# Attention and two MLPs on one core: the first MLP's first tile takes ten steps of d_ff before tile two, not six

## The chip, the cores and the metric

One NeuronCore of a Trainium2 chip runs the whole program in one launch. The metric is device microseconds of that core, from launch to end. A profile is one execution with the hardware profiler on.

## What is computed

For 4 batches and 8 heads of 768 positions and 64 dimensions, each chunk of 32 queries attends to 16 positions to its left, its own 32, 8 to its right, and 8 memory positions. The result, as 3072 tokens of 512 values, goes through two MLPs with d_ff = 2048:

```python
scores = scale * np.matmul(q_c, k_full.transpose(0, 1, 3, 2))
a = softmax(scores); out[:, :, c_start:c_end] = np.matmul(a, v_full)
...
h = x @ w_in                                    # first MLP
g = np.where(h > 0.0, h, alpha * (np.exp(np.minimum(h, 0.0)) - 1.0))
x = g @ w_out
...
r = np.maximum(x @ w_in2, 0.0)                  # second MLP
out = (s * (r * r) + b) @ w_out2
```

## The kernel before, in words

**Attention** is cut into 24 units of 128 queries (all heads at once), numbered here from 0 as in the code; the fifth to the eighth are units 4 to 7. For a unit u < 8, step S multiplies q and k (tile psS, L239) and runs the softmax on VectorE and ScalarE (L258 to L266), step P turns the probabilities round on TensorE (psP, L281) into the one tile pt, and step V multiplies them by v (psV, L313) and splits the result into a high and a low part of the first MLP's input: xh (ScalarE, L204) and xl (VectorE, L208). From unit 8 on P is a series of transposes on VectorE (L289), and V of one unit and S of the next share one PSUM tile (psVS). Once the first MLP has begun, psS, psV and psVS come from one and the same PSUM slot (`ps_a`, one buffer): S of unit u+2 cannot start before xl of unit u has been read out of psV.

**The first MLP** works on 6 tiles of 512 tokens (4 units each). All products are three matmuls of rounded parts (L361, L362, L363: high by high, high by low, low by high). A step (t, c) of tile t takes the c-th of 16 blocks of 128 of d_ff: 12 matmuls into psH (first layer, `h1`), then ELU (L392, L393 on ScalarE, L394 on VectorE), the split into gh (L204) and gl (L208), and two steps later 12 matmuls into the four accumulators acc (`out1`). Tile 0 is taken in two pieces: its first `HF` steps come as soon as units 0 to 3 are done, then all 16 steps of tile 1, then the rest of tile 0. Between the pieces the four accumulators of tile 0 are copied out, stored to a scratch tensor (`part_dram`, L427), and later loaded (L413) and added to (L419).

**Weights** come as float64. Each of the 32 loads (raw, L149, 512 KB) is turned into high and low parts by four operations, two on ScalarE (top L158, w L172) and two on VectorE (t L161, w L208). `weights_to` doles these out as micro-steps between the parts of a step.

**Order.** The first steps, up to V of unit 3, stand in a table written by hand (EARLY) and are held in that order. After it, `mlp1_step` writes a step of the MLP and, with `beside`, the next few attention steps and weight micro-steps; the framework then schedules each engine's instructions by its own cost model, and each engine runs its list in order. The list `steps` has 73 attention steps: S0, then S, P, V of each unit to 7 (three per unit), then three per unit. `ready[0]` is 14 and `ready[1]` is 26, so 13 attention steps, from S of unit 5 to P of unit 8, are spread over the first piece of tile 0. The 47 that are left are spread from step (1, `ATT_FROM`) to (3, 8). All loads and stores go through one queue, SP's, in order; a load that waits for its buffer holds up those behind it.

Of the kernel before, what the change touches and what calls it, by code (L numbers as in the profile page):

```python
# [28 lines left out]
NU = B * UPB  # L29
NP = H // 2  # L30
NU0 = 8
HF = 6
ATT_FROM, ATT_END = 10, (3, 8)
MICRO = 8
HN, NT2 = 512, 3
NBLOCK = 10
# [25 lines left out]
def tile_attention_then_two_mlps(ctx, tc, q_in, k_in, v_in, w1, w2, s_in, b_in, out):  # L62
# [270 lines left out]
    def load_x(t):  # L333

        X[t] = xh, xl = x_tiles((t + 1) % 2)
        nc.sync.dma_start(out=f(xl), in_=x_dram[:, :, starts[t] * U:(starts[t] + sizes[t]) * U])
        nc.scalar.activation(out=xh, in_=f(xl), func=AF.Copy)
        sub(xl, f(xl), xh)
# [47 lines left out]
    def h1(t, c):  # L386
        n = sizes[t] * U
        n0 = 2 * U if t == 0 and c in HALF else 0
        ps = HALF.pop(c) if n0 else ps_h.tile([P, 512], F32, tag="h", name="psH")
        h_mm(c, ps, X[t], n0, n)  # L390
        g = one.tile([P, MAXN], F32, tag="g", name="g")
        nc.scalar.activation(out=g[:, :n], in_=ps[:, :n], func=AF.Relu, scale=-1.0)  # L392
        nc.scalar.activation(out=g[:, :n], in_=g[:, :n], func=AF.Exp, scale=-1.0)  # L393
        nc.vector.scalar_tensor_tensor(out=g[:, :n], in0=g[:, :n], scalar=-1.0, in1=ps[:, :n],  # L394
                                       op0=ALU.add, op1=ALU.max)
        G[1, t, c] = split_g(g, n)
# [10 lines left out]
    def put_out(t, c, n):  # L407

        split, t0 = t == 0, starts[t] * U
        if c == HF and split:  # L410
            for m in range(KT):
                PART[m] = big_tile(n, m == 3)
                nc.sync.dma_start(out=PART[m], in_=part_dram[:, m, :n])  # L413
        if c == NF - 1 or c == HF - 1 and split:
            for m, acc in enumerate(ACC[t]):
# [13 lines left out]
    def out1(t, c):  # L429
        n = sizes[t] * U  # L430
        first, last = (c in (0, HF), c in (HF - 1, NF - 1)) if t == 0 else (c == 0, c == NF - 1)
        if first:
# [41 lines left out]
    def prepare_all():  # L474
        for layer in range(2):
            for i in range(NF // 2):
                yield from prepare(layer, i)
# [17 lines left out]
    ready = [min(next(k for k, g in enumerate(steps) if g and g[0] in ((step_V, u), (step_VS, u))) + 2, len(steps)) for u in last_v]  # L495
# [21 lines left out]
    def run_step(group):  # L517
        for st, u in group:
            s = u + (st is step_VS)
            while st in (step_S, step_VS) and nload[0] <= min(s + 1, NU - 1):  # L520
                load_qk(nload[0])
                nload[0] += 1
            while st in (step_S, step_VS) and nload[1] <= s:
                load_v(nload[1])
                nload[1] += 1
            st(u)
# [10 lines left out]
    def weights_to(w, n, ahead):  # L537

        while wnext[0] < min(n, MICRO * NF):
            k, m = divmod(wnext[0], MICRO // 2)  # L540
            load_ws(w, k + 1 + ahead)
            if m == 0:
                wsteps[:] = [split_w(*SLOTS[k], wraw[k])]
            next(wsteps[0])
            wnext[0] += 1
# [40 lines left out]
    def beside(want, weights):  # L586

        w, n, ahead = weights
        n0, d0 = wnext[0], done[0]
        while done[0] < want:  # L590
            run_step(steps[done[0]])
            done[0] += 1
            weights_to(w, n0 + (n - n0) * (done[0] - d0) // (want - d0), ahead)
        weights_to(w, n, ahead)
# [48 lines left out]
    def open_second():  # L643

        z = (NTILE1 + 1) % 2
        halves = iter(range(10))
        for j in (1, 2, 3, 6, 5, 7, 4):
            if j in (6, 5):
                xc = xp.tile([P, 2, 2, HN], F32R, tag=f"{'xh' if j == 6 else 'xl'}{z}", name=f"xc{j}")
                XC[j] = xc[:, 0], xc[:, 1]  # L650
            else:
                XC[j] = high(next(halves)), high(next(halves))
        p2["yr"] = [wps[1].tile([P, 2, HN], F32, tag=f"w1_{c}", name=f"yr{c}") for c in range(4)]
        p2["blocks"] = load_blocks(0)

    def mlp1_step(n_):

        t, c = seq[n_]
        phase[0] = (1 if c < HF else 3) if t == 0 else 2 if t == 1 else 4

        a0, total, k, ks = done[0], 0, 0, 1
        if t == 0 and c < HF:
            a0, total, k, ks = ready[0] - 1, ready[1] - ready[0] + 1, c, HF
        elif spread[0] <= n_ < spread[1]:
            a0, total, k, ks = ready[1], len(steps) - ready[1], n_ - spread[0], spread[1] - spread[0]

        wt = [(w1, 0, 4)] * 2
        if t == 0 and c < HF:
            n0, n1 = 12, 8 * HF + 12
            wt = [(w1, max(n0 + (n1 - n0) * (2 * c + z) // (2 * HF), MICRO * (c + z) - 4), 4) for z in (1, 2)]  # L670
        elif t == 1:
            n0 = 8 * HF + 12
            wt = [(w1, max(n0 + (MICRO * NF - n0) * (2 * c + z) // 28, MICRO * (c + z) - 4), 4) for z in (1, 2)]
        if (t, c) == ATT_END:
            actx.close()
            op.append(mctx.enter_context(tc.tile_pool(name="op2", bufs=2)))
            p2["prep"] = mctx.enter_context(tc.tile_pool(name="prep", bufs=2, reuse_waits="tile"))
            p2["steps"] = prepare_all()
            nc.sync.dma_start(out=s_sb, in_=s_in.to_broadcast([P, 1]))
            nc.sync.dma_start(out=b_sb, in_=b_in.to_broadcast([P, 1]))  # L680
        if t < 2:
            weights_to(w1, MICRO * c + 4, 4)
        if t == NTILE1 - 1 and c == NBLOCK:
            open_second()
        h1(t, c)
        yield
        beside(a0 + total * (2 * k + 1) // (2 * ks), wt[0])
        prepared(t, 2 * c + 1)
        yield
        beside(a0 + total * (2 * k + 2) // (2 * ks), wt[1])  # L690
        prepared(t, 2 * c + 2)
        if t == NTILE1 - 1 and c >= NBLOCK:
            for _ in range(3):
                next(p2["blocks"], None)
        if c == NF - 4 and 1 <= (t or 1) < NTILE1 - 1 and t != 1:
            assert done[0] >= ready[max(t, 1) + 1]
            load_x(max(t, 1) + 1)
        yield

    def prepared(t, n):  # L700

        begin = 2 * (NF * ATT_END[0] + ATT_END[1])
        want = min(NPREP * (2 * NF * t + n - begin) // (2 * NF * (NTILE1 - 1) + 2 * NBLOCK - 2 - begin), NPREP)
        while (t, n) > (ATT_END[0], 2 * ATT_END[1]) and p2["n"] < want:
            next(p2["steps"])
            p2["n"] += 1
# [7 lines left out]
    def single(n_):  # L714
        step = mlp1_step(n_)
        next(step)
        next(step)
        if n_ >= 2:
            out1(*seq[n_ - 2])
        next(step)  # L720

    def pair(n_):
        steps2 = [mlp1_step(n_), mlp1_step(n_ + 1)]
        for k in (0, 0, 1, 0):
            next(steps2[k])
        for k in range(2):
            out1(*seq[n_ - 2 + k])
            next(steps2[1])
# [185 lines left out]
```

## Time and profile before

| | us |
|---|---|
| median of 3 runs | 1088.03 |
| the runs | 1088.59, 1088.03, 1078.59 |
| the profiled execution | 1087.85 |
| its span, first to last instruction | 1086.1 |
| TensorE busy in the span | 1062.0 |

In a row of the trace the times are microseconds from the start of the span. A group gives the start, the time to the end of its last instruction, the engine, the line, the operation, and how many there are; a bracket gives the time for which the engine had stood idle, and what ended it. Matmul durations overlap: the work of a run of matmuls is read from start to start. PEclk is the granted clock of TensorE, 1.00 for 2.4 GHz and 0.50 for 1.2 GHz.

### The profile page before, as it was taken

To read this page: it belongs to the slowest core of one execution; us is meant where nothing else is said; L and a number is where in the kernel's file an instruction comes from. 1 tells how busy PE (TensorE), PEld (TensorE's weight loads), DVE (VectorE), ACT (ScalarE), POOL (GpSimd) and SP (SyncE) were. 2 spreads that over 40 slices of the span, in tenths; PEclk is the share of its full clock that TensorE was granted. 3 is DMA by queue.
4 is the path that set the end of the run, shared out by engine and by line. 5 is a ranking of instruction groups with operands and counts; after the bars stand their busy time and mean duration, and the time that the engine had idled before them with its cause. 6 is when DMAs were issued, how large, how long until landed. Compare 5 with 4: busy or idle time off the path is not lost.

```text
span 1086.1 us, 18733 instructions
## 1 busy us (share of the span) xinstructions
PE 1062.0 (98%) x7466; PEld 865.4 (80%) x7466; DVE 731.9 (67%) x1133; ACT 548.2 (50%) x773; POOL 1.2 (0%) x7
## 2 busy tenths in 40 slices
PE   6899999999999999999999899999999999999998
PEld 5778888878888888888878787788888788888887
DVE  6788558777778777787773155697356696365854
ACT  3677533443434356676763255654355654355542
POOL 0000000000000000000000000000000000000000
PEclk7799999999999999999999999999999999999999
DMA  8886025516325158988932366767766777666673
GB/s 314 333 309 219 11 63 161 177 59 191 109 79 178 50 170 309 334 318 314 332 131 78 126 193 188 245 201 232 231 192 186 243 214 228 208 195 193 201 206 126
DMA packets 94838, 213.02 MB, mean 196 GB/s; under 512 B 9760, under 2 KB 17952, under 8 KB 92704
## 3 DMA queue, kind: packets, MB, share of 16 engines
q1 hardware_dynamic: 94176, 210.79, 60.3%
q8 instruction: 59, 0.97, 0.4%
q10 hardware_dynamic: 576, 1.05, 0.3%
q14 instruction: 27, 0.22, 0.1%
HBM read 164.61 MB, written 47.19 MB: 195 GB/s over the span
## 4 chain that ended last, share of the span: by engine, by line
PE 80%; DVE 9%; DMA 5%; ACT 3%; issue 2%; SPq 0%; ACTq 0%; DVEq 0%
PE psH L361 13%; PE psH L363 12%; PE psH L362 12%; PE psL L362 7%; PE psL L363 7%; PE psL L361 7%; PE acc L361 6%; PE acc L362 6%; PE acc L363 6%; DVE pt L289 2%; DMA hi<-y_dram 2%; DMA raw<-w 1%; DVE g L394 1%; DVE gl L208 1%; PE psVS L313 1%
## 5 line engine op out<-in xcount | busy, mean ns | idle before, releaser
L361 PE MATMUL psH<-xh,w 128*128 128x512 f32 (+1 forms) x392 | 154.8, 395 | 2.3 <-ACT xh L204 1.2
L363 PE MATMUL psH<-xh,w 128*128 128x512 f32 (+1 forms) x392 | 152.4, 389 | 0.0
L362 PE MATMUL psH<-xl,w 128*128 128x512 f32 (+1 forms) x392 | 152.0, 388 | 0.2 <-DVE xl L208 0.2
L361 PE MATMUL acc<-gh,w 128*128 128x512 f32 x384 | 152.0, 396 | 0.0
L362 PE MATMUL acc<-gl,w 128*128 128x512 f32 x384 | 150.7, 392 | 0.0
L363 PE MATMUL acc<-gh,w 128*128 128x512 f32 x384 | 150.5, 392 | 0.0
L394 DVE SCALAR_TENSOR_TENSOR g<-g,psH 128x512 f32<-128x512 f32 x96 | 65.7, 684 | 62.4 <-ACT g L393 61.5
L392 ACT ACTIVATE g<-psH 128x512 f32<-128x512 f32 x96 | 56.7, 591 | 94.0 <-PE psH L363 51.4
L204 ACT ACTIVATE gh<-g 128x512 fp32r<-128x512 f32 x96 | 60.3, 628 | 84.6 <-DVE g L394 84.3
L361 PE MATMUL psH<-hi,hi 128*128 128x512 f32 x240 | 94.0, 398 | 1.3 <-ACT p L765 1.3
L362 PE MATMUL psH<-hi,hi 128*128 128x512 f32 x240 | 93.8, 391 | 0.0
L363 PE MATMUL psH<-hi,hi 128*128 128x512 f32 x240 | 93.7, 390 | 0.0
L815 ACT ACTIVATE g2xl<-g 128x1024 fp32r<-128x1024 f32 x56 | 59.5, 1063 | 60.1 <-PE psL L363 59.9
L361 PEld LDWEIGHTS psH<-xh,w 128*128 128x128 f32 x392 | 74.4, 190 | 18.8 <-ACT xh L204 1.6
L362 PE MATMUL psL<-g2l,hi 128*128 128x512 f32 x224 | 87.4, 390 | 1.2 <-DVE g2l L208 1.2
L208 DVE TENSOR_TENSOR gl<-g,gh 128x512 fp32r<-128x512 f32 x96 | 66.2, 690 | 32.1 <-ACT gh L204 30.5
L363 PE MATMUL psL<-g2xl,hi 128*128 128x512 f32 x224 | 87.1, 389 | 0.0
L362 PEld LDWEIGHTS psH<-xl,w 128*128 128x128 f32 x392 | 74.6, 190 | 15.6 <-DVE xl L208 0.6
L361 PE MATMUL psL<-g2xl,hi 128*128 128x512 f32 x224 | 86.8, 389 | 0.0
L363 PEld LDWEIGHTS psH<-xh,w 128*128 128x128 f32 x392 | 74.3, 190 | 15.5
L361 PEld LDWEIGHTS acc<-gh,w 128*128 128x128 f32 x384 | 72.6, 189 | 16.7 <-ACT pt L204 0.6
L363 PEld LDWEIGHTS acc<-gh,w 128*128 128x128 f32 x384 | 72.5, 189 | 15.7
(108 smaller groups left out, 1847.3 us busy)
## 6 DMA issues: line engine op xcount, KB each, us to landing
hi<-s_dram SPq DMA_DIRECT2D x336, 256.0 KB, 3.0
raw<-w SPq DMA_DIRECT2D x64, 511.8 KB, 6.3
s_dram<-right SPq DMA_DIRECT2D x16, 1024.0 KB, 5.2
kb<-k SPq DMA_DIRECT2D x24, 512.0 KB, 5.7
v<-v SPq DMA_DIRECT2D x24, 512.0 KB, 3.8
s_dram<-left SPq DMA_DIRECT2D x16, 768.0 KB, 4.1
q<-q SPq DMA_DIRECT2D x24, 256.0 KB, 5.3
out<-r SPq DMA_DIRECT2D x24, 256.0 KB, 3.7
```

What stands on the lines that cost most here:

```text
L204: return nc.scalar.activation(out=hi, in_=src, func=AF.Copy)
L208: return nc.vector.tensor_tensor(out=lo, in0=src, in1=f(hi), op=ALU.subtract)
L289: nc.vector.transpose(out=pt[k * CH:(k + 1) * CH, :, rows], in_=sm[rows, :, z, n0:n0 + CH])
L313: keep(nc.tensor.matmul(ps[r % 2 * D:(r % 2 + 1) * D, z, o:o + CH], v[rows, (r * NC + c) * D:(r * NC + c + 1) * D], pt[rows, r, cs], start ...
L361: keep(nc.tensor.matmul(o, sa(a[0]), sb(b[0]), start=first, stop=False, skip_group_check=again))
L362: keep(nc.tensor.matmul(o, sa(a[0]), sb(b[1]), start=False, stop=False, skip_group_check=again))
L363: return keep(nc.tensor.matmul(o, sa(a[1]), sb(b[0]), start=False, stop=last, skip_group_check=again))
L392: nc.scalar.activation(out=g[:, :n], in_=ps[:, :n], func=AF.Relu, scale=-1.0)
L394: nc.vector.scalar_tensor_tensor(out=g[:, :n], in0=g[:, :n], scalar=-1.0, in1=ps[:, :n], op0=ALU.add, op1=ALU.max)
L815: nc.scalar.activation(out=gh, in_=g[:, block], func=AF.Copy)
```

## The change

Tile 0's first piece has ten steps, not six (`HF` is also the number at which its accumulators are put out and begun again), and its second piece six, not ten. The 13 attention steps beside the first piece are spread over nine of its steps (`ks` is `HF - 1`; `min` keeps the tenth from asking for more). The 47 others begin at step 4 of tile 1, not at step 10; that is 42 MLP steps to spread over in place of 40. The weight micro-steps per MLP step are the same (8), and the target of the first piece rises from 60 to 92 of the 128.

```diff
-HF = 6
-ATT_FROM, ATT_END = 10, (3, 8)
+HF = 10
+ATT_FROM, ATT_END = 4, (3, 8)
...
         if t == 0 and c < HF:
-            a0, total, k, ks = ready[0] - 1, ready[1] - ready[0] + 1, c, HF
+            a0, total, k, ks = ready[0] - 1, ready[1] - ready[0] + 1, c, HF - 1
...
-        beside(a0 + total * (2 * k + 1) // (2 * ks), wt[0])
+        beside(a0 + min(total * (2 * k + 1) // (2 * ks), total), wt[0])
         prepared(t, 2 * c + 1)
         yield
-        beside(a0 + total * (2 * k + 2) // (2 * ks), wt[1])
+        beside(a0 + min(total * (2 * k + 2) // (2 * ks), total), wt[1])
```

What stands where now is seen from the scheduled lists. On TensorE, between V of unit 4 (psV) and V of unit 5, there stood before (psH of w_3 is tile 0's step 3, acc of w_0 its step 0; a run of 12 matmuls is cut to its ends):

```order
L363 MATMUL psH<-xh,w_2_686 128x512
L313 MATMUL psV<-pt,v 64x32 x32
L361 MATMUL psH<-xh,w_2_686 128x512
L362 MATMUL psH<-xl,w_2_686 128x512
L363 MATMUL psH<-xh,w_2_686 128x512
L239 MATMUL psS<-kb,q 32x64 x32
L281 MATMUL psP<-ident,sm_106 128x128 x4
L361 MATMUL psH<-xh,w_3_765 128x512
L362 MATMUL psH<-xl,w_3_765 128x512
L361 MATMUL acc_866<-gh,w_0_602 128x512
...
L363 MATMUL acc_869<-gh,w_0_602 128x512
L313 MATMUL psV<-pt,v 64x32 x32
```

and now:

```order
L313 MATMUL psV<-pt,v 64x32 x32
L361 MATMUL acc_810<-gh,w_0_602 128x512
...
L363 MATMUL acc_813<-gh,w_0_602 128x512
L361 MATMUL psH<-xh,w_3_728 128x512
...
L363 MATMUL psH<-xh,w_3_728 128x512
L239 MATMUL psS<-kb,q 32x64 x32
L361 MATMUL psH<-xh,w_3_728 128x512
L362 MATMUL psH<-xl,w_3_728 128x512
L363 MATMUL psH<-xh,w_3_728 128x512
L281 MATMUL psP<-ident,sm_106 128x128 x4
L361 MATMUL acc_810<-gh,w_1_694 128x512
```

Before, three large matmuls stood between V of unit 4 and S of unit 6; now 21 do (12 of acc, 9 of psH). Further on, 12 stand between V of unit 5 and S of unit 7, 11 between V of unit 6 and S of unit 8, and 35 between V of unit 7 and the first matmul of tile 1, where before two of that tile's matmuls came after five.

On SP's queue, from the load of unit 4's v on, before:

```order
L199 DMA v<-v 128x1024
L192 DMA kb<-k 128x1024
L194 DMA q<-q 128x512
L199 DMA v<-v 128x1024
L149 DMA raw_1_675<-w 128x2047
L149 DMA raw_3_677<-w 128x2047
L149 DMA raw_2_679<-w 128x2047
L149 DMA raw_4_681<-w 128x2047
L149 DMA raw_3_695<-w 128x2047
```

and now:

```order
L199 DMA v<-v 128x1024
L149 DMA raw_1_625<-w 128x2047
L149 DMA raw_3_627<-w 128x2047
L149 DMA raw_2_629<-w 128x2047
L149 DMA raw_4_631<-w 128x2047
L192 DMA kb<-k 128x1024
L194 DMA q<-q 128x512
L199 DMA v<-v 128x1024
L149 DMA raw_3_689<-w 128x2047
```

Four weight loads have moved ahead of k and q of unit 6 and v of unit 5.

## Rows read from the trace of the kernel before

**Rows 1.** Page, part 1: busy time, share of the span, instructions.
```profile
PE 1062.0 (98%) x7466; PEld 865.4 (80%) x7466; DVE 731.9 (67%) x1133; ACT 548.2 (50%) x773; POOL 1.2 (0%) x7
```

**Rows 2.** Busy time by stretch: stretch, length, each engine, granted clock, DMA share, GB/s.
```profile
0.00:39.15 39.15, 30.86 (x726) 25.87 (x727) 24.26 (x47) 15.97 (x26) 1.16 (x7) 0.78 0.85 296
39.15:55.16 16.01, 13.05 (x222) 9.69 (x222) 13.91 (x27) 10.99 (x19) 0.00 (x0) 0.79 0.96 381
55.16:81.12 25.96, 24.66 (x352) 19.07 (x346) 22.34 (x42) 19.19 (x33) 0.00 (x0) 1.00 0.84 315
81.12:560.00 478.88, 477.46 (x3933) 391.70 (x3932) 352.30 (x708) 250.51 (x401) 0.00 (x0) 1.00 0.53 182
560.00:645.00 85.00, 81.17 (x347) 65.62 (x346) 34.83 (x42) 33.11 (x49) 0.00 (x0) 0.98 0.37 112
645.00:1086.00 441.00, 434.82 (x1897) 353.47 (x1896) 284.27 (x271) 218.43 (x247) 0.00 (x0) 1.00 0.70 205
```

**Rows 3.** Timeline of TensorE, 41 to 62 us.
```profile
41.39 1.14 PE L313 MATMUL psV<-pt,v 64*64 64x32 f32 x64
...
45.07 0.76 PE L239 MATMUL psS<-kb,q 64*32 64x64 f32 x52 [1.65 <-DVE xl L208]
47.13 0.46 PE L239 MATMUL psS<-kb,q 64*32 64x64 f32 x12 [1.30 <-issue]
47.52 1.11 PE L281 MATMUL psP<-ident,sm 128*128 128x128 f32 x4
48.28 0.78 PE L361 MATMUL psH<-xh,w 128*128 128x512 f32 x1
...
53.33 0.39 PE L361 MATMUL acc<-gh,w 128*128 128x512 f32 x1
...
54.10 1.14 PE L313 MATMUL psV<-pt,v 64*64 64x32 f32 x64
55.16 0.50 PE L363 MATMUL psH<-xh,w 128*128 128x512 f32 x1
...
57.65 0.86 PE L239 MATMUL psS<-kb,q 64*32 64x64 f32 x64
58.44 0.50 PE L361 MATMUL acc<-gh,w 128*128 128x512 f32 x1
...
61.30 0.60 PE L281 MATMUL psP<-ident,sm 128*128 128x128 f32 x4
61.65 0.48 PE L361 MATMUL psH<-xh,w 128*128 128x512 f32 x1
```

**Rows 4.** Busy time by stretch, columns as in rows 2.
```profile
44.00:46.00 2.00, 0.76 (x52) 0.60 (x52) 2.00 (x5) 0.89 (x2) 0.00 (x0) 1.00 1.04 411
46.00:48.00 2.00, 0.87 (x15) 0.70 (x15) 1.06 (x4) 1.66 (x4) 0.00 (x0) 0.62 1.02 391
48.00:50.00 2.00, 2.00 (x7) 1.35 (x7) 2.00 (x4) 1.87 (x4) 0.00 (x0) 0.50 1.04 417
```

**Rows 5.** Timeline of TensorE, around the first matmuls of tile 1, and later.
```profile
79.21 0.73 PE L361 MATMUL psH<-xh,w 128*128 128x512 f32 x2 [1.15 <-ACT xh L204]
...
80.55 0.50 PE L362 MATMUL psH<-xl,w 128*128 128x512 f32 x1 [0.15 <-DVE xl L208]
...
95.04 0.39 PE L361 MATMUL acc<-gh,w 128*128 128x512 f32 x1
...
100.51 0.39 PE L361 MATMUL psH<-xh,w 128*128 128x512 f32 x1
```

**Rows 6.** Timeline of VectorE: xl of units 4 to 7.
```profile
44.37 0.64 DVE L208 TENSOR_TENSOR xl<-psV,xh 128x512 fp32r<-128x512 f32 x1
...
55.93 0.69 DVE L208 TENSOR_TENSOR xl<-psV,xh 128x512 fp32r<-128x512 f32 x1 [1.01 <-ACT xh L204]
...
67.61 0.68 DVE L208 TENSOR_TENSOR xl<-psV,xh 128x512 fp32r<-128x512 f32 x1
...
79.80 0.69 DVE L208 TENSOR_TENSOR xl<-psV,xh 128x512 fp32r<-128x512 f32 x1
```

**Rows 7.** Timeline of TensorE: V of units 6 and 7, and unit 13's.
```profile
64.58 1.14 PE L313 MATMUL psV<-pt,v 64*64 64x32 f32 x64
...
75.57 1.13 PE L313 MATMUL psV<-pt,v 64*64 64x32 f32 x64
...
225.13 0.78 PE L313 MATMUL psVS<-pt,v 64*64 64x32 f32 x38 [1.10 <-DVE pt L289]
```

**Rows 8.** Timeline of SP's queue: k and q of unit 6, v of unit 5.
```profile
30.33 0.33 SPq L192 DMA_DIRECT2D kb<-k  x1
30.71 0.42 SPq L194 DMA_DIRECT2D q<-q  x1
33.46 0.33 SPq L199 DMA_DIRECT2D v<-v  x1
33.84 3.54 SPq L149 DMA_DIRECT2D raw<-w  x6
```

**Rows 9.** DMA queue 8 between 44 and 45 us: packets, MB, share of 16 engines.
```profile
q8 instruction: 1, 0.02, 6.7%
```

**Rows 10.** DMA issues: tile, queue, count, KB each, median us to landing.
```profile
big<-part SPq DMA_DIRECT2D x4, 256.0 KB, 3.6
```

**Rows 11.** Timeline of VectorE: two instructions back to back, a transpose group.
```profile
49.13 0.68 DVE L208 TENSOR_TENSOR w<-t,w 128x512 fp32r<-128x512 f32 x1
49.73 0.68 DVE L259 TENSOR_TENSOR sm<-psS,nmx 128x512 f32<-128x512 f32 x1
...
80.53 3.79 DVE L289 STREAM_TRANSPOSE pt<-sm 32x128 f32<-32x128 f32 x12
```

## The prediction

> **What bounds the kernel now.** I read first the busy times: TensorE works 1062.0 us of 1086.1 us [rows 1], so a change that only moves work can give back at most 24.1 us of idle time, and what lies in half-clock stretches. Then the same by stretch, to see where those lie [rows 2]. Of the idle time 39.15 - 30.86 = 8.3 us comes before the first full 512-column matmul, 3.0 us from there to V of unit 4 being followed by V of unit 5 (39.15 to 55.16), 1.3 us to the first step of tile 1, 1.4 us in the long middle, and 10.0 us after 560 us, where the second MLP is being opened and run. The change touches the second and third stretch and the order in the fourth. The lists of the engines are the same before V of unit 4 but for details, and the same again from tile 2 on, so the first stretch and the last two should stand. Two things make up the second stretch: idle time and clock. Its granted clock is 0.79, while the next is at 1.00 [rows 2].
>
> The timeline of TensorE shows the chain there [rows 3]. S of unit 6 waits 1.65 us for xl of unit 4, because only three large matmuls lie between V of unit 4 and it, and VectorE gets to xl at 44.37 us, 1.84 us after V's end at 42.53 [rows 3, 6]. In the middle of S comes another pause, 1.30 us, put down to issue. Behind the two the granted clock falls from 1.00 to 0.50, by way of 0.62 [rows 4], and stays there until 53.33 us.
>
> **What the change takes away, step by step.**
>
> The wait for xl of unit 4: xl ends at 45.01 us, 2.5 us after V. Now 21 large matmuls stand between V and S. One takes 0.228 us at full clock: from 95.04 to 100.51 us lie 24 of them [rows 5], 5.47 / 24. So 21 are 4.8 us, against 2.5 us: **1.65 us** gone.
>
> The half clock: from 48.28 to 53.33 us eleven matmuls take 5.05 us; at 0.228 they take 2.51 us, so 2.5 us. The four transposes of P take 0.76 us from start to start (47.52 to 48.28) against 0.35 us at full clock (61.30 to 61.65): 0.4 us. S takes 45.07 to 47.52, less 1.30 us, which is 1.15 us, against 0.79 us (57.65 to 58.44): 0.35 us [rows 3]. If TensorE does not stop before S, nothing like that fall should follow: **3.2 us**.
>
> The first matmuls of tile 1 wait 1.15 us for xh of unit 7 and 0.15 us for xl [rows 5]. They stood a few matmuls behind V of unit 7; xl of that unit ends at 80.49 us, 3.8 us after V's end at 76.70 us [rows 6, 7], since VectorE was busy with the transposes of unit 8. Now 35 matmuls, 8.0 us, are between: **1.3 us** gone.
>
> The pause of 1.30 us in S of unit 6: one packet of instructions is fetched between 44 and 45 us [rows 9], with the DMA engines at a share of 1.04 [rows 4], and the pause begins right behind. S is 64 short matmuls with as many weight loads, so nothing long stands in the queue to cover a late fetch. The matmuls that now come ahead of S move such a border within S but not out of it, and the weights are still being loaded then. Nothing excludes that it comes again (0 us gained), nor that the steadier stream hides it (1.30 us gained). I take half, **0.65 us**; other groups of S show no such pause. The Trainium skill speaks to this ("Runtime: NRT & Kernel Launch", section "Instruction fetch mechanics"): an engine fetches the next block of 256 instructions by itself while it runs the present one, and crossing a border is "mostly hidden". The row shows a pause that is not hidden, if it is one of these. By the page the pause would go altogether, and the sum below would be 0.65 us lower; by the row alone it would be 0.65 us higher.
>
> Together 1.65 + 3.2 + 1.3 + 0.65 = 6.8 us.
>
> **What it adds or moves.**
>
> The two other handovers of the PSUM slot: S of unit 7 now has 12 matmuls ahead (2.74 us), S of unit 8 has 11 (2.5 us). From V's end to xl's end it took 1.4 us in unit 5 (55.24 to 56.62) and 2.6 us in unit 6 (65.72 to 68.29) [rows 3, 6, 7]. So unit 8 may wait some 0.1 us, and either waits if VectorE is later than there. From below the cost is 0, from above it is what S of unit 6 paid. I take the near end, **0.3 us** for both.
>
> Four weight loads ahead of k and q of unit 6 and v of unit 5. They are 4 x 0.512 = 2.05 MB; at the 381 GB/s of that stretch [rows 2] they hold back what follows by 5.4 us. k of unit 6 is issued at 30.33 us, v of unit 5 at 33.46 us [rows 8]; S of unit 6 would now begin at about 48 us and V of unit 5 at about 55 us. Nothing; the weights themselves come several us earlier than in the row of six at 33.84 us, which is a help to VectorE. Later groups of four loads follow each V, and the steps that want them are at least two behind.
>
> VectorE in tile 0's first piece. TensorE's work from step 2 to tile 1 is 192 large matmuls (43.8 us), four V at 1.06 us (54.10 to 55.16), three S at 0.79 us and three P at 0.35 us, together 51.5 us. The change's list for VectorE from the ELU of step 0 to that of step 9 has 74 instructions of full size, 9 small ones and 16 transposes. Back to back a large one takes 0.60 us, a transpose 3.79 / 12 = 0.32 us [rows 11]; with 0.15 us for a small one (an estimate, between these starts) that is 44.4 + 1.4 + 5.1 = 51 us. So VectorE is as long as TensorE here. It was so before (22.34 of 25.96 us busy, 86% [rows 2]), without holding TensorE anywhere but at the two handovers. What TensorE needs from it first, the weights of the next steps, comes before the transposes in the list. I put nothing, and make it a rival.
>
> Tile 0's second piece is now six steps. Its partial sums must be back before its last step: five steps of 24 matmuls are 27 us, a load lands in 3.6 us [rows 10]. Hidden. The pause of 1.10 us at V of unit 13, behind the transposes [rows 7], lies where the end of tile 0 and attention meet; they meet again, so I keep it, with -1.1 to +1.1 us as its bounds.
>
> **The sum.** -6.8 + 0.3 = -6.5 us, against the profiled execution's 1087.85 us: 1081.35 us. The median is 0.18 us above that execution, so **1081.5 us**. One of the three runs before is 0.9% below the others (1078.59); so I take 1%, 10.9 us, as about what a measurement of this kernel can tell from no change: below 1077.2 us is faster, above 1098.9 us is slower.
>
> **The rivals.**
>
> *VectorE becomes the bound of tile 0's first piece.* If it stays busy only 86% of the time, as in the stretch before tile 1, its 51 us take 59 us. It begins at about 39 us, with the ELU of step 0, and so ends at 98 us; tile 1's second group of psH, which needs the bank that step 9's ELU frees, would begin at 39.15 + 51.5 + 2.7 = 93.4 us. TensorE waits 4.6 us, spread over several steps: 1086 us, and 1088 us with one stretch of lower clock. For it: the 51 us. Against: its idle time before was mostly time in which TensorE, too, was late. Chance 0.24.
>
> *The handovers turn against it (slower).* In place of one S, all three wait: units 7 and 8 as unit 6 did, each 1.65 us, its fetch 1.30 us, and its half clock 3.2 us. Unit 6's stays as well, and tile 1's 1.3 us go: 2 x 6.15 - 1.3 = +11.0 us, 1099 us. It decides by whether xl ends more than 2.74 us (unit 5) and 2.5 us (unit 6) after V by over 1.5 us; three more VectorE instructions ahead of xl would do it. Against: for unit 6 it took 2.6 us with VectorE just as full. Chance 0.07.
>
> *More falls away than I count.* The run at 1078.59 us shows that 9.4 us can go with no change at all; where, no trace shows. The first 39 us hold the largest idle time and a clock of 0.78 [rows 2]. If the changed kernel is mostly in that condition: 1081.5 - 9.4 = 1072 us. Chance 0.13.
>
> That the change does not do what it says is ruled out by the scheduled lists: the 21 matmuls and the four earlier weight loads are there.
>
> **The numbers.** The forecast, 1078 to 1085 us, has 0.56; VectorE as the bound, 1085 to 1091 us, 0.24; more falling away, 1069 to 1078 us, 0.13; the handovers, 1091 to 1100 us, 0.07. The range 1074 to 1091 us leaves out the last and about half of the third. Faster by over 1%: 0.13, nearly all of the third. Slower by over 1%: 0.05, most of the last. Within 1%: 0.82.
>
> **What would show it.** In the profile after: no idle time before S of unit 6, a granted clock of 1.00 from about 39 us on, no wait at tile 1's first psH, which should begin near 91 us, and V of unit 4 and the stretches after 560 us as before. A wait of psS for xl at units 7 or 8, or of psH and acc for w, gl or g between 50 and 100 us, would mean the handovers or VectorE. It is wrong altogether if the half clock comes back without a pause, or if the first 39 us change.

## The result and the profile after

The changed kernel takes 1076.14 us (median of 8 runs, 1074.13 to 1077.32), the kernel before 1085.41 us in the same comparison (8 runs, 1078.59 to 1088.66): a ratio of 0.9914 [0.9895, 0.9933] (the brackets are the 95% interval), 9.3 us less. The forecast was 6.5 us less, from a kernel before of 1088.03 us. In microseconds 1076.14 lies inside the stated range, but outside the forecast's own 1078 to 1085 us: it is among the times of the third rival, more falling away. Of the 5.4 us to the forecast's 1081.5 us, 2.6 us are the lower median of the kernel before; the other 2.7 us are gain that was not forecast. The two profiled executions lie further apart than the medians, with spans of 1086.1 and 1072.3 us: that of before is near the upper end of its runs, that of after is the lowest of its own.

Busy time in the changed kernel (part 1 of the page, answers to [rows 1]): TensorE's share is 98% as before, of a span that is 13.8 us shorter.

```profile
PE 1055.4 (98%) x7466; PEld 860.1 (80%) x7466; DVE 733.4 (68%) x1135; ACT 546.7 (51%) x771; POOL 1.2 (0%) x7
```

Busy time by stretch in the changed kernel, columns as in [rows 2]; the first two stretches are the same, the others are laid about the same work (546 to 631 us here is what [rows 2] have from 560 to 645 us):

```profile
0.00:39.15 39.15, 30.36 (x731) 24.91 (x732) 26.18 (x50) 17.72 (x29) 1.16 (x7) 0.87 0.93 347
39.15:55.16 16.01, 16.01 (x217) 12.62 (x218) 15.05 (x30) 13.42 (x25) 0.00 (x0) 1.00 0.90 354
55.16:91.00 35.84, 35.17 (x438) 27.86 (x432) 31.91 (x61) 26.37 (x46) 0.00 (x0) 1.00 0.82 312
...
546.00:631.00 85.00, 84.29 (x369) 68.53 (x368) 36.83 (x44) 35.34 (x52) 0.00 (x0) 1.00 0.37 111
```

From 39.15 to 55.16 us TensorE does not stop, and its clock is 1.00 where it was 0.79. But the stretch of the second MLP has changed too: 0.7 us idle out of 85, where [rows 2] have 3.8. That was not forecast.

The timeline of TensorE in the changed kernel, answering to [rows 3, 5]:

```profile
41.01 1.14 PE L313 MATMUL psV<-pt,v 64*64 64x32 f32 x64
42.07 0.50 PE L361 MATMUL acc<-gh,w 128*128 128x512 f32 x1
...
47.10 0.86 PE L239 MATMUL psS<-kb,q 64*32 64x64 f32 x64
47.89 0.50 PE L361 MATMUL psH<-xh,w 128*128 128x512 f32 x1
...
58.77 0.86 PE L239 MATMUL psS<-kb,q 64*32 64x64 f32 x64
...
66.33 0.50 PE L361 MATMUL psH<-xh,w 128*128 128x512 f32 x1 [0.29 <-DVE g L394]
...
69.27 1.14 PE L313 MATMUL psV<-pt,v 64*64 64x32 f32 x64
...
73.06 0.86 PE L239 MATMUL psS<-kb,q 64*32 64x64 f32 x64
...
80.72 0.50 PE L361 MATMUL psH<-xh,w 128*128 128x512 f32 x1 [0.39 <-DVE g L394]
...
83.67 1.14 PE L313 MATMUL psV<-pt,v 64*64 64x32 f32 x64
...
92.89 0.39 PE L361 MATMUL psH<-xh,w 128*128 128x512 f32 x1
```

S of unit 6 (47.10) is one run of 64 with no bracket, and the full clock goes on behind it (0.79 us to the next matmul). S of units 7 and 8 (58.77 and 73.06) have none either. The first psH of tile 1 (92.89) has none. The two brackets left, 0.29 and 0.39 us for g, are the only waits of this stretch. VectorE in the same kernel, xl of units 4 to 7, answering to [rows 6]:

```profile
45.06 0.69 DVE L208 TENSOR_TENSOR xl<-psV,xh 128x512 fp32r<-128x512 f32 x1
...
57.59 0.68 DVE L208 TENSOR_TENSOR xl<-psV,xh 128x512 fp32r<-128x512 f32 x1
...
71.73 0.68 DVE L208 TENSOR_TENSOR xl<-psV,xh 128x512 fp32r<-128x512 f32 x1
...
86.72 0.68 DVE L208 TENSOR_TENSOR xl<-psV,xh 128x512 fp32r<-128x512 f32 x1
```

xl ends 1.35 us ahead of S of unit 6, 0.50 us ahead of S of unit 7 and 0.65 us ahead of S of unit 8.

The pause inside S went, too, and the fetch of instructions shows how. [rows 9] have one between 44 and 45 us; it begins at 44.66 us, while TensorE stands and waits for xl, and the pause ends 2.47 us later. In the changed kernel a fetch begins at 43.33 us:

```profile
q8 instruction: 1, 0.02, 6.8%
```

That is 3.77 us ahead of S, with large matmuls still to run. (The row is DMA queue 8 from 43 to 44 us.) In x1 and x10 below, with 11 large matmuls ahead of S and not 21, fetches begin at 43.54 and 43.40 us, and short pauses are left in S that end 2.50 and 2.49 us later. So what hides a fetch here is the work that TensorE has in hand when it begins; this is read from the traces, no run changed it by itself.

Where the 13.8 us of the two profiled executions lie, by the starts of the same instructions: 1.9 us ahead of the first 512-column matmul (39.15 before, 37.20 after), 6.9 us from there to 560 us, 4.9 us from there to 640 us. The first part is not shown to be the kernel's: that matmul began at 39.15 and 37.36 us in two profiles of the kernel before (x4 below), at 37.20 and 35.77 us in two of the changed one (x8). The pauses of TensorE put down to issue in these first 39 us came and went from run to run; the one in V of unit 2 was 0.43 us in x5, with the order of before, and 2.02 us in x7, with the order of after. The middle part is what the forecast was about.

Of the late part, 1.2 us is a wait for g at 566 us that the second profile of the kernel before does not have and the second of the changed one has (1.05 us). The other 3.7 us are one pause and the low clock behind it. It stands at TensorE's first matmul of the second MLP that needs a free PSUM bank again. In the kernel before:

```profile
619.63 0.56 PE L361 MATMUL psH<-xc,hi 128*128 128x512 f32 x1 [2.76 <-ACT m L765]
```

and in the kernel after:

```profile
607.40 0.50 PE L361 MATMUL psH<-xc,hi 128*128 128x512 f32 x1 [0.71 <-ACT m L765]
```

Behind the long one TensorE's clock is 0.50 for 3.5 us (620.1 to 623.6 us), about 1.6 us more. It is so in x6 and x9 as well, but in x2, x3, x4 and x7, with pauses of 2.5 to 2.9 us at the same place, the clock stays at 1.00. ScalarE's timeline shows what m waits for, and SP's what stands beside it. Before, ScalarE, then SP, then TensorE's last matmul on the last gl of the first MLP:

```profile
611.61 0.34 ACTq L427 DMA_DIRECT2D y_dram<-big  x1
...
612.41 1.68 ACTq L427 DMA_DIRECT2D y_dram<-big  x3
618.98 0.60 ACT L765 ACTIVATE m<-psH 128x512 f32<-128x512 f32 x1 [6.04 <-DMA y_dram<-big]
```

```profile
612.79 0.37 SPq L628 DMA_DIRECT2D yr<-y_dram  x1
```

```profile
612.37 0.39 PE L362 MATMUL acc<-gl,w 128*128 128x512 f32 x1
```

After, ScalarE, then SP, then TensorE's last matmul on the gl of the step before the last:

```profile
601.43 0.34 ACTq L427 DMA_DIRECT2D y_dram<-big  x1
...
602.22 1.73 ACTq L427 DMA_DIRECT2D y_dram<-big  x3
606.75 0.60 ACT L765 ACTIVATE m<-psH 128x512 f32<-128x512 f32 x1 [4.00 <-DMA y_dram<-big]
```

```profile
599.88 0.37 SPq L628 DMA_DIRECT2D yr<-y_dram  x1
```

```profile
599.47 0.39 PE L362 MATMUL acc<-gl,w 128*128 128x512 f32 x1
```

m is written where `big` lay and waits for the last four stores of y, which go through ScalarE's queue. (That all loads and stores go through SP's is true of the other tiles, not of the last.) Before, the 512 KB load yr is issued in the middle of these stores, and they are done 4.9 us after the last issue (614.09 to 618.98); after, it is issued 1.55 us ahead of the first store, and they are done in 2.8 us (603.95 to 606.75). The load has to wait because yr shares SBUF with a `gl` buffer of the first MLP. In the kernel before it leaves 0.03 us behind the end of the last matmul on the last step's gl, in the changed one 0.02 us behind the end of the last matmul on the gl of the step before, which stands 12 matmuls earlier. The change has swapped which of the two buffers comes last; nothing in the diff speaks of it.

### The profile page after: what moved, and what is told of

Same layout as the page of the kernel before. It is cut to its first block, busy times and chain, and to the rows that moved or that the text cites. A ratio compares the mean times of both kernels' runs of the same rounds, so it can differ in the third digit from the quotient of the medians.

```text
span 1072.3 us, 18728 instructions
## 1 busy us (share of the span) xinstructions
PE 1055.4 (98%) x7466; PEld 860.1 (80%) x7466; DVE 733.4 (68%) x1135; ACT 546.7 (51%) x771; POOL 1.2 (0%) x7
## 3 DMA queue, kind: packets, MB, share of 16 engines
q10 hardware_dynamic: 576, 1.05, 0.3%
## 4 chain that ended last, share of the span: by engine, by line
PE 83%; DVE 7%; DMA 5%; ACT 3%; issue 2%; SPq 0%; ACTq 0%; DVEq 0%
PE psH L361 14%; PE psH L363 13%; PE psH L362 13%; PE psL L362 7%; PE psL L363 7%; PE acc L361 6%; PE psL L361 6%; PE acc L362 6%; PE acc L363 6%; DMA hi<-y_dram 2%; DVE pt L289 2%; DMA xl<-x_dram 1%; DVE g L394 1%; PE psVS L313 1%; PE psV L313 1%
```

## The experiments

Two theories. **A**: the gain is the time around S of unit 6 (the wait for xl, the pause in S and the half clock behind them) and the wait of tile 1's first matmuls, as forecast. **T**: a part is the yr load. The rivals: that the weights came too late before (W), that the condition of the run made the difference (C), and that how thin attention is spread (D) or the earlier start of the later units (L) counts for itself. All ratios are to the kernel before, with runs of both on the same chip.

**x1_late6**, the place of S of unit 6 without the ten steps: the kernel before, with attention beside the first piece one attention step later.

```diff
+        late = t == 0 and c < HF
-        beside(a0 + total * (2 * k + 1) // (2 * ks), wt[0])
+        beside(a0 + max(total * (2 * k + 1) // (2 * ks) - late, 0), wt[0])
...
-        beside(a0 + total * (2 * k + 2) // (2 * ks), wt[1])
+        beside(a0 + total * (2 * k + 2) // (2 * ks) - (late and c < HF - 1), wt[1])
```

> The kernel before (six steps) with one edit: beside tile 0's first piece the attention steps come one later, so that S of unit 6 has 11 large matmuls ahead of it and not 3; tile 1's first matmuls still stand 5 behind V of unit 7. Theory A (the wait at S of unit 6 and the half clock behind it are most of the gain, tile 1's first wait the rest): no pause before that S, granted clock 1.00 from there on, the wait of about 1.3 us at tile 1 stays or grows; 5.5 us faster than before (ratio 0.995), so 1080 beside a before of 1085. Theory L (the length of the piece or the earlier start of the later units matters): no faster than before. Theory C (the gain is mostly chance, how the clock happens to fall): a spread of runs like before's, 1078 to 1089.

0.9939 [0.9917, 0.9960]. Timeline of TensorE in this kernel, the places of [rows 3, 5]:

```profile
44.98 0.66 PE L239 MATMUL psS<-kb,q 64*32 64x64 f32 x40
46.04 0.43 PE L239 MATMUL psS<-kb,q 64*32 64x64 f32 x24 [0.41 <-issue]
...
72.98 0.73 PE L361 MATMUL psH<-xh,w 128*128 128x512 f32 x2
...
86.59 0.50 PE L361 MATMUL psH<-xh,w 128*128 128x512 f32 x1 [1.63 <-DVE g L394]
```

With 11 matmuls ahead S of unit 6 does not wait for xl, the pause in it is 0.41 us, and the clock stays at 1.00 from 39 to 91 us. Tile 1's first matmuls (72.98 us) do not wait for xh or xl either, though they stand five matmuls behind V of unit 7 as before; three steps on TensorE waits 1.63 us for g, for which VectorE first had 16 transposes of unit 8 to do (74.35 to 79.39 us). So A's first part is shown without the ten steps. Its yr load came early too, though (605.96 us, the pause for m 1.07 us), so the 0.61% is not A's alone; and four weight loads left earlier, at 27.20 us, as in the changed kernel (25.85 us).

**x2_dense10**, the changed kernel with the 13 attention steps beside six steps again, not nine.

```diff
-            a0, total, k, ks = ready[0] - 1, ready[1] - ready[0] + 1, c, HF - 1
+            a0, total, k, ks = ready[0] - 1, ready[1] - ready[0] + 1, c, 6
```

> The changed kernel with one edit: ten steps in tile 0's first piece, but the 13 attention steps crowded beside the first six, as before. S of unit 6 has 3 large matmuls ahead again; tile 1's first matmuls stand far behind V of unit 7. Theory A: the wait before S of unit 6 (1.7 us), a pause within it and the half clock (3.2 us) are back, tile 1's wait is gone; 1 to 2 us faster than before (ratio 0.998 to 0.999). Theory L: as fast as the changed kernel, 0.991.

0.9973 [0.9955, 0.9990]. The timeline of TensorE, then the stretch of the handover (columns as in [rows 2]):

```profile
43.67 0.96 PE L239 MATMUL psS<-kb,q 64*32 64x64 f32 x52 [1.58 <-DVE xl L208]
45.74 0.45 PE L239 MATMUL psS<-kb,q 64*32 64x64 f32 x12 [1.10 <-issue]
...
615.20 0.50 PE L361 MATMUL psH<-xc,hi 128*128 128x512 f32 x1 [2.88 <-ACT m L765]
```

```profile
39.15:55.16 16.01, 13.32 (x226) 9.95 (x225) 13.74 (x27) 11.69 (x20) 0.00 (x0) 0.79 0.91 349
```

The wait, the pause and the half clock are back as in [rows 3], so ten steps alone do not do it; the spread over nine does. The yr load is late as well (608.24 us, in the middle of the stores), and the long pause with it: two things go back at once, and the 0.59% between this kernel and the changed one belong to both. x6 below parts them.

**x3_ahead8**, the kernel before with weights up to 8 micro-steps ahead, not 4 (the third argument of the tuples in `wt` and of `weights_to`).

```diff
-        wt = [(w1, 0, 4)] * 2
+        wt = [(w1, 0, 8)] * 2
...
-            weights_to(w1, MICRO * c + 4, 4)
+            weights_to(w1, MICRO * c + 4, 8)
```

> The kernel before with weight loads issued eight ahead in place of four; order on TensorE around S of unit 6 as before. Theory A: no change, ratio 0.998 to 1.002, the wait before S of unit 6 is there. Rival W (the change gains because its weight loads go out earlier, at 27 us in place of 34 us): several us faster, with VectorE earlier at xl of unit 4.

1.0001 [0.9987, 1.0016]; S of unit 6 waits 1.64 us for xl, as before. But the edit does not do what W needs: the first of its weight loads behind unit 5's v leaves at 33.93 us, as before (33.84 us, [rows 8]), only with more loads in a row behind it; the changed kernel has four at 25.85 us. So x3 leaves W untested. The trace of the changed kernel answers it for the wait: xl ends 3.60 us behind V there, not 2.48 us as before, so earlier weights did not bring it forward, and behind three large matmuls (0.7 us) S would have waited longer than before. In x1 and x10, where weights leave early as well, it ends 1.4 us behind V, sooner than before but still later than three matmuls would cover.

**x4_before_again**, the kernel before once more, for a second profile.

> The kernel before, unchanged, for a second profile. Theory A: the wait of 1.65 us before S of unit 6 and tile 1's 1.3 us are there again, since the order makes them. Theory C: they are not, or differ by as much as they cost. The pauses at 24 us, at 566 us and at 617 us (2.1, 1.1 and 2.8 us in the first profile) show whether the 2 us by which the measured gain exceeds the forecast belong to stretches that the change does not touch: if they vary between two profiles of one kernel, they do.

1083.98 us, one run. S of unit 6 waits 1.60 us for xl and pauses 1.54 us, tile 1's first psH waits 1.15 us, the pause for m is 2.75 us: these four are the kernel's. The pause in V of unit 2 varies (1.61 us, 2.14 before), and the one for g at 566 us (1.08 us before) is not there.

**x5_before_yr_up**, the kernel before with 4 KB of unused SBUF ahead of yr, so that yr lies over another gl.

```diff
+    pad = yrp.tile([P, 2, HN], F32, tag="pad", name="pad")
+    nc.vector.memset(pad[:1, 0, :1], 0.0)
     p2["yr"] = [yrp.tile([P, 2, HN], F32, tag=f"yr{k}", name=f"yr{k}") for k in range(4)]
```

> The kernel before, with the four yr tiles of the second MLP (loaded for its tile 1 while the first MLP ends) placed 4 KB a partition further on. They then lie over the buffer of gl that the last step but one reads, as in the changed kernel, and not over the last step's, as in the kernel before. Theory T (part of the measured gain is this side effect at 600 to 620 us, far from the edit: the changed kernel swaps two gl buffers, so the yr load starts 12 matmuls, 2.7 us, earlier and no longer collides with the last stores that ScalarE waits for): the pause of 2.8 us at the second MLP's start falls to about 0.7 us; 2 to 4 us faster than before (ratio 0.996 to 0.998), the wait at S of unit 6 stays. Theory A alone (all the gain is at units 4 to 7): no change, ratio 0.999 to 1.001.

0.9973 [0.9959, 0.9987]. Timelines of SP and of TensorE:

```profile
607.19 0.37 SPq L628 DMA_DIRECT2D yr<-y_dram  x1
```

```profile
615.05 0.50 PE L361 MATMUL psH<-xc,hi 128*128 128x512 f32 x1 [1.05 <-ACT m L767]
```

The load leaves 1.54 us ahead of the first store (608.73 us), the pause falls from 2.76 to 1.05 us, and S of unit 6 still waits (1.10 us, and a pause of 1.31 us). T is shown: about 0.27%, 2.9 us, with no change of order on TensorE.

**x6_after_yr_up**, the changed kernel with the same two lines.

> The changed kernel with the same shift of the yr tiles; there it puts them over the gl buffer that the last step reads. Theory T: the pause of 2.8 us is back, 2 to 4 us slower than the changed kernel, ratio to before 0.993 to 0.996. Theory A alone: as the changed kernel, 0.991.

0.9939 [0.9919, 0.9960]. The pad now moves yr onto the last gl; TensorE's timeline has the long pause again, and the handover is untouched:

```profile
47.00 0.86 PE L239 MATMUL psS<-kb,q 64*32 64x64 f32 x64
...
609.18 0.69 PE L361 MATMUL psH<-xc,hi 128*128 128x512 f32 x1 [2.66 <-ACT m L767]
```

The same lines that made the kernel before faster make the changed one slower, by 0.31 points against its second timing (x8). What is left, 0.6%, is the change without T. And beside x2, which has the late load as well, x6 shows the handover by itself: the two differ in the spread of the 13 steps (and the pad), and by 0.34 points, 3.7 us.

**x7_after_yr_clear**, the changed kernel with two such pads (8 KB), meant to free the load of both buffers.

```diff
+    pads = [yrp.tile([P, 2, HN], F32, tag=f"pad{k}", name=f"pad{k}") for k in range(2)]
+    for pad in pads:
+        nc.vector.memset(pad[:1, 0, :1], 0.0)
```

> The changed kernel with the yr tiles 8 KB a partition further on, clear of all gl buffers, so that their load can go as soon as SP's queue reaches it. Theory T: the last 0.7 us of the pause go too; 0 to 1.5 us faster than the changed kernel, ratio 0.990. Theory A alone: 0.991.

A miss: 0.9932 [0.9917, 0.9948]. The load left at 608.15 us, behind the first store (606.02 us), and TensorE paused 2.48 us for m, as T has it for a load among the stores; it also waited some 3.0 us for g in all, 0.7 us of them beside tile 0's first piece. The load left right behind VectorE's last copy of acc into `big` (607.44 us, 0.69 us) and the two writes to the pads (608.08 us), not behind a matmul on gl. Which of these it waited for was not separated.

**x8_after_again**, the changed kernel once more.

> The changed kernel, unchanged, on the same chip as the three others, and for a second profile. Ratio 0.990 to 0.993 to before. The early pause in V of unit 2 (0.4 us in its first profile, 1.6 to 2.1 us in four profiles of kernels whose first 24 us have the same order) shows whether that difference goes with the kernel (0.4 us again) or with the run (1.6 us or more, and a half-clock stretch behind it).

1074.64 us, 0.9908 [0.9892, 0.9923]; the pause for m 1.18 us, no wait at S, the two waits for g of 0.30 and 0.39 us again, and a third of 1.05 us at 556 us, which the first profile does not have. The pause in V of unit 2 was 1.08 us, between what the two theories expected, and decides nothing.

**x9_from4**, the kernel before with the later attention begun at step 4 of tile 1.

```diff
-ATT_FROM, ATT_END = 10, (3, 8)
+ATT_FROM, ATT_END = 4, (3, 8)
```

> The kernel before with only the other half of the edit: units 9 and on spread from tile 1's step 4, not 10; six steps in tile 0's first piece. S of unit 6, tile 1's first matmuls and the yr load stand as before. Theory A with T: ratio 0.998 to 1.001, with what the pauses before V of units 9 to 15 (1.4 us in the first profile) may give. Theory L (a good part of the gain is the earlier start of the later units): 0.993 to 0.996.

A miss, between the two expectations: 0.9967 [0.9952, 0.9982], some 3.6 us less, with S of unit 6 waiting (0.85 us, a pause of 1.85 us) and the long pause for m (2.75 us) both in place. TensorE by stretch in this kernel (columns as in [rows 2]):

```profile
91.00:250.00 159.00, 159.00 (x1650) 130.50 (x1650) 119.43 (x254) 72.63 (x120) 0.00 (x0) 1.00 0.41 130
250.00:400.00 150.00, 150.00 (x1550) 122.82 (x1549) 104.94 (x236) 62.76 (x100) 0.00 (x0) 1.00 0.35 110
```

Not a moment idle in 309 us, while before it waited 1.42 us for pt there (the 1.10 us at 225.13 us, [rows 7], and 0.32 us later; 2.2 us in x4). So 1.4 to 2.2 of the 3.6 us are located; the rest is not.

**x10_hf8** and **x11_hf12**, the changed kernel with 8 and with 12 steps in the first piece.

```diff
-HF = 10
+HF = 8
```

> The changed kernel with eight steps in tile 0's first piece (attention beside seven). S of unit 6 has 11 large matmuls ahead, tile 1's first stand 36 behind V of unit 7, yr lies over the last step but one's gl. Theory A with T: all three terms are gained, as with ten: ratio 0.990 to 0.993. Theory D (what counts is how thin attention is spread): half of the gain, 0.994 to 0.996.

> The changed kernel with twelve steps in tile 0's first piece (attention beside eleven); 12 large matmuls ahead of S of unit 6, more behind V of unit 7. Theory A with T: nothing left to gain there, ratio 0.990 to 0.993. Theory D: more than ten steps, 0.987 to 0.989.

0.9898 [0.9880, 0.9915] and 0.9925 [0.9906, 0.9943]. Eight is as good as ten: S of unit 6 pauses 0.33 us and waits for nothing. Twelve gains nothing more: TensorE waits three times for g, 1.7 us in all, and for pt 1.5 us. D, by which eight would give half the gain and twelve more than ten, falls.

**x12_after_from9**, the changed kernel with the later attention begun at step 9 (with 10 the units of tile 2 would not be done in time).

```diff
-ATT_FROM, ATT_END = 4, (3, 8)
+ATT_FROM, ATT_END = 9, (3, 8)
```

> The changed kernel with the 47 later attention steps begun at step 9 of tile 1 (next to the 10 of the kernel before; 10 itself leaves too few steps for tile 0's ten), not at step 4. Tile 0's first piece and the late yr load are as in the changed kernel. If the 0.33% that the start at step 4 alone gave in the kernel before (x9) is the waits of TensorE for pt at V of the later units, which came to 1.4 and 2.2 us there in two profiles, 0 at a start at step 4, and 0.6 and 0.4 us in the two profiles of the changed kernel: such waits come back to 1.4 us or more between 91 and 400 us, and the ratio to the kernel before is 0.9915 to 0.994, some 1 to 3 us above the changed kernel. If the 0.33% was the scatter of the first 39 us or the pause in S of unit 6, and the start of the later attention is worth nothing: ratio 0.989 to 0.9915, as the changed kernel's 0.9908, and waits between 91 and 400 us of under 1 us. By both: no wait of S of unit 6 for xl, full clock from 39 to 91 us, and a wait for m at the second MLP of about 1 us.

1.0032 [1.0015, 1.0049], slower than before, far beyond both expectations: 1087.75 against 1085.02 us. The handover is as in the changed kernel (S of unit 6 a run of 64, clock 1.00 from 39 to 91 us, the pause for m 1.20 us). The loss lies between 220 and 240 us (columns as in [rows 2]):

```profile
220.00:230.00 10.00, 7.21 (x33) 5.60 (x31) 7.02 (x15) 4.73 (x8) 0.00 (x0) 1.00 0.20 55
230.00:240.00 10.00, 7.35 (x136) 5.84 (x136) 7.38 (x18) 2.96 (x5) 0.00 (x0) 0.66 0.28 80
```

The timelines of SP, ScalarE, VectorE and TensorE in this kernel show the chain:

```profile
203.40 0.52 SPq L329 DMA_DIRECT2D x_dram<-xs  x1
204.01 3.37 SPq L413 DMA_DIRECT2D big<-part  x3
208.19 0.58 SPq L336 DMA_DIRECT2D xl<-x_dram  x1
```

```profile
216.34 1.92 ACT L337 ACTIVATE xh<-xl 128x2048 fp32r<-128x2048 f32 x1 [5.28 <-DMA xl<-x_dram]
...
223.83 0.58 ACT L204 ACTIVATE xs<-psVS 128x512 f32<-128x512 f32 x1
```

```profile
218.29 2.29 DVE L208 TENSOR_TENSOR xl<-xl,xh 128x2048 fp32r<-128x2048 f32 x1 [3.95 <-ACT xh L337]
```

```profile
229.75 0.27 PE L313 MATMUL psVS<-pt,v 64*64 64x32 f32 x2 [2.79 <-issue]
230.35 0.31 PE L313 MATMUL psVS<-pt,v 64*64 64x32 f32 x6 [0.34 <-DVE pt L289]
231.72 0.30 PE L313 MATMUL psVS<-pt,v 64*64 64x32 f32 x2 [1.05 <-DVE pt L289]
```

The store of the last unit of tile 2 goes out at 203.40 us, the load of that tile's x must come behind it, and tile 0's partial sums are loaded between the two. ScalarE stands 5.28 us for x and VectorE 3.95 us behind it, with the next unit's softmax queued behind both; its pt is late, and TensorE waits over 5 us (the 2.79 us are put down to issue, but end 0.7 us after VectorE has begun pt, at 229.04 us) and runs at 0.50 for some 7 us. In the changed kernel the load of x leaves at 184.57 us, 21 us ahead of the first load of the sums, and ScalarE waits 1.18 us for it. So the start at step 4 is worth some 13 us beside ten steps (0.9908 against 1.0032), and 3.6 us beside six. Of the 13 us the waits of TensorE between 229 and 235 us make 5.4 and the low clock about 2.8; the rest is not located. The chain is read from the timelines; no run moved the loads of the sums alone.

## Why the prediction came out right, point by point

**The wait for xl (1.65 us) and the half clock (3.2 us).** Confirmed: x1 takes them away without the change, x2 brings them back in it. In the profiled run xl was later behind V than forecast (3.6 us from V's end at 42.15 us, not 2.5), and the matmuls covered that too: S began 4.95 us behind V's end. By x2 and x6 the whole handover, with the pause in S, is worth 3.7 us; the sum had 5.5 us (1.65 + 3.2 + 0.65). The intervals, 0.2 points either way in each run, leave room for the difference.

**The pause in S of unit 6 (half of 1.30 us).** It went whole: no pause in x8, x6 or after, 0.33 us in x10. It is there with 1.1 to 1.9 us in the five further profiled runs with the wait (x2, x3, x4, x5, x9). That agrees, at this place, with the Trainium skill ("Runtime: NRT & Kernel Launch", section "Instruction fetch mechanics"), by which the cost of a border is "mostly hidden". It is not so for V of units 2 and 3, also groups of short matmuls: in the changed kernel's profile V of unit 3 paused 1.62 us. The half that I left in was 0.65 us too careful.

**Tile 1's first matmuls (1.3 us).** Gone in after, x6 and x8, and in x2, x7, x10, x11 and x12; 1.1 to 1.2 us in x4, x5 and x9, 0.8 us in x3. But it is gone in x1, too, with five matmuls and not 35 behind V of unit 7: there ScalarE came to xh sooner, 0.7 us behind V. So that the 35 matmuls are what takes it away is not shown; x1 has the wait for g in its place.

**The two other handovers (+0.3 us).** They cost nothing; xl is 0.50 and 0.65 us ahead. The slower rival, that all three would wait, falls with them: for it xl would have had to come 1.5 us behind the turn of S.

**VectorE as the bound.** Two waits for g, 0.29 and 0.39 us, against the 4.6 us of the rival. With twelve steps there were two near the piece, 0.54 and 0.50 us (x11); no more than a sign of it.

**What failed: "the same again from tile 2 on, so the first stretch and the last two should stand."** The lists of instructions are nearly the same there, but what their tiles lie over is not. The yr load was worth 2.9 us by x5 and about as much by x6 against x8, and it is about what the forecast of -6.5 us lacks of the measured -9.3 us. I counted places in queues and left out where buffers are put in SBUF. So the third rival's time came, but only in part by its cause: the condition of the first 39 us is in the profiled pair and not shown to be the kernel's, the yr load is a mechanism that no rival had. The prediction named a change in the first 39 us as a sign against itself; it came (1.9 us of the profiled pair), but the start of the first full matmul differs by 1.8 us between two profiles of the kernel before.

**What was right by luck.** The forecast kept the pause for pt at 225 us, with -1.1 to +1.1 us as its bounds, whatever `ATT_FROM` is. Between 91 and 400 us the waits for pt came to 0 to 1.1 us with a start at step 4 (1.5 us with twelve steps, x11), and to 1.4 to 2.2 us with a start at 10; with ten steps and a start at 9 they grow to 5.4 us in one place, with a stretch of half clock behind. The short second piece of tile 0 brings the loads of its sums up to the load of tile 2's x on SP's queue; this price I hid under "Hidden", asking whether the sums come in time and not what they hold up. The start at step 4, which I gave no term, avoids it. Luck also lies in the total, as far as the intervals tell: the handover came out smaller than its terms, the earlier start of the later units gave something that had no term, and the two about cancel.

**What stays open.** A chain of kernels splits the gain. From before to x2 (ten steps and the start at step 4, without the handover and with the late load) it is 0.27%, which is tile 1's first wait and what the later attention gives; from x2 to x6, the handover, 0.34 points; from x6 to x8, the yr load, 0.31 points. Each step has an interval of 0.2 to 0.3 points either way, so the sizes are rough, and they need not be the same in another order. x9's traces explain only half of its gain, and x12's about 8 of 13 us. No version was clearly better than the changed kernel; x10 is its equal.

## What to carry to other kernels

Where one buffer is handed from step to step, count the other work between its reader and its next writer, and give it more than the reader's delay in a busy run (here 3.6 us). The wait itself was the smaller part of the cost here: 1.65 us, with a pause of 1.30 us beside it and 3.2 us of lower clock behind both. When a change only reorders, ask of each load in the kernel, also far from the change, which buffer it lies over and who reads that last. And of a load that is hidden itself, ask what stands behind it on its queue.

## What the runs showed of the hardware

**Fetches of instructions.** A pause of TensorE put down to issue ended 2.2 to 2.5 us after a fetch of instructions had begun, in all 40 such pauses of the first 50 us of the fourteen profiles (as in [rows 9], the fetch at 44.66 us and the pause that ends at 47.13). The pauses were 0.25 to 2.2 us long, from run to run of one kernel. The profile of the kernel before has 59 such fetches on this queue for 14,932 matmuls and weight loads.

**The clock.** It fell to 0.50 in all six profiles in which S of unit 6 waited and paused (2.4 to 3.2 us idle in the two together). It fell behind three of the seven long pauses for m (2.5 to 2.9 us), and not behind the other four; here the kernel before, which ran at it for 3.5 us, and x2, which did not:

```profile
620.00:623.00 3.00, 3.00 (x9) 2.32 (x8) 0.30 (x1) 0.64 (x2) 0.00 (x0) 0.50 0.00 0
```

```profile
616.00:619.00 3.00, 3.00 (x14) 2.36 (x13) 0.00 (x0) 1.09 (x2) 0.00 (x0) 1.00 0.35 89
```

So the length of a pause alone does not tell whether the clock falls.

**Stores beside a load.** Four stores of 256 KB took 4.6 to 5.0 us from the last issue to the instruction that waits for them in the seven profiles in which a 512 KB load was issued among them, and 2.8 to 3.5 us in the seven in which it was issued ahead of them.
